# A gated recurrence that feeds a max-out feed-forward layer: the opening rearranged, the last rows stored by two queues

## The chip, the cores and the metric

The kernel runs on one core of a Trainium2 chip. The metric is device time in microseconds of one execution. Five executions of the kernel before took 400.87 to 401.7 us, median 401.0. The core's engines are TensorE (PE in the profile; PEld is its weight load), VectorE (DVE), ScalarE (ACT), GpSimd (POOL) and SyncE (SP). Each engine runs its own instructions in order. 16 DMA engines move data; transfers are issued by SP, ACT or POOL.

## The reference, cut to what matters

```python
# x, f_logit: (4, 6144, 256); lower_bound: (256)
f = lower_bound + (1 - lower_bound) * sigmoid(f_logit)
i = 1 - f
for t in range(6144):                      # for each of 4 batches
    h = f[:, t] * h + i[:, t] * x[:, t]
    y[:, t] = h
X = y.reshape(24576, 256)
out = np.maximum(X @ w1, X @ w2) @ w_out   # w1, w2: (256, 1024), w_out: (1024, 256)
```

All inputs and the output are float32.

## The kernel before

**Algebra.** With om = 1 - lower_bound and u = sigmoid(-f_logit), the forget factor is 1 - om·u and the input is om·u·x. The kernel scans with u·x as the drive, so the scan gives h/om, and folds om into the weights. The maximum is written as h1 + relu(h2 - h1): `wd` is om·(w2 - w1) in bf16, `rt` is relu(y·wd), and the output is rt·w_out + y·w13, where w13 = om·(w1·w_out) is a 256x256 matrix that the kernel computes in its opening. For that it needs w1 turned (`w1T`): `turn_w1` turns a quarter (256 of 1024 columns) by four TensorE transposes into PSUM, and `keep_w1` copies the quarter to SBUF as bf16.

**Tiling.** The 24576 tokens are 48 blocks of 512. For a block, 8 `hidden` steps (fc = 0 to 7) make one 128-column slice of y·wd each (two matmuls 128x512 into a PSUM tile `dT`) and evacuate it by a relu on ScalarE or VectorE. `project` then adds, for four groups of 128 tokens, 8 matmuls with `rt` and 2 with `y` into a PSUM tile `psO`; `store` copies two groups to SBUF (`osb`) and issues the output transfer on SP. In the main loop block j's hidden steps alternate with block j-1's project steps.

**Getting u, x and y turned.** The recurrence runs along the free dimension, so inputs must lie with channels on partitions. Blocks 0 to 2 are loaded as they are (`load`, tiles `fn`, `xn`), gated by ScalarE (`gate_nat`, `un`), multiplied by VectorE (`drive_nat`, `vn`) and turned by TensorE (`turn_pe`, PSUM tiles that come from the same pool of five as the hidden tiles). From block 3 on, chunks (block 3 alone, then pairs) are cast to bf16 into DRAM by DMAs issued on POOL (`cast`: `fs`, `xs`), turned by transposing DMAs issued on SP (`turn_dma`: `fT`, `xT`), gated by ScalarE (`gate`) and driven by VectorE (`drive`). `forget` makes the factors `ff` (ScalarE or VectorE), `scan` makes y (VectorE). Order between chunks: POOL copies one element of the last thing it must wait for into `held` and then issues the next cast. So the first cast waits for block 2's `fn` load (L520), and each later cast for the `fT` transpose of the chunk before (L389).

**The order around the change.** The order is written out by hand (`manual_schedule`), one list that gives each engine's order. The opening, L397 to L523, runs: loads on SP (weights by quarters, `w_out` by halves, blocks 0 to 2) and one load on ACT; a few filler matmuls (`keep_warm`); block 0 in two halves of 256 tokens, with the weight preparation quarter by quarter between (`diff` = w2 - w1 on POOL or VectorE, `scale` by om on ScalarE, `turn_w1`, `keep_w1`); block 1 in two halves; `linear_weights` and `keep_linear` for w13. The main loop from L525 starts with j = 1; within it block 2 is still gated, turned and scanned, between block 1's hidden steps (L537 to L551), block 0 is stored, and `gate_of` and `turn_of` say at which (block, step) a later block is gated and a chunk's transposes are issued.

**The end.** The last two groups of 128 tokens have a PSUM tile of their own; `store_row` copies half of the columns by VectorE and half by ScalarE into one tile and issues one transfer on SP.

Of the kernel before, what the change touches and what calls it, by code (L numbers as in the profile page):

```python
# [8 lines left out]
FP32 = mybir.dt.float32  # L9
# [7 lines left out]
def kernel(  # L17
# [42 lines left out]
    ypool = ctx.enter_context(tc.tile_pool(name="ypool", bufs=4))  # L60
    rpool = ctx.enter_context(tc.tile_pool(name="rpool", bufs=2 * FC + 4))
    opool = ctx.enter_context(tc.tile_pool(name="opool", bufs=4))
    PS = bass.MemoryType.PSUM
    ps_d = ctx.enter_context(tc.tile_pool(name="ps_d", bufs=5, space=PS))
    ps_o = ctx.enter_context(tc.tile_pool(name="ps_o", bufs=3, space=PS))
# [6 lines left out]
    nom = const.tile([P, KC], FP32)  # L72
    lbr = const.tile([KC, P], FP32)
    w1n = wpool.tile([P, KC, DFF], FP32)
    w2n = wpool.tile([P, KC, DFF], FP32)
    wdf = wpool.tile([P, KC, DFF], FP32)
    won = wpool.tile([P, FC, D], FP32)
# [13 lines left out]
    def load(j, s, q0, q1, eng=nc.sync):  # L91
        src = (f_logit, x)[s]
        eng.dma_start(
            out=ins[j][s][:, q0:q1, :],
            in_=src[0, j * TB + q0 * P : j * TB + q1 * P, :].rearrange(
                "(q p) d -> p q d", p=P
            ),
        )
# [18 lines left out]
    def turn_pe(j, s, q):  # L117
        if q == 0:
            (uT, vT)[s][j] = ps_d.tile([P, KC, TB], BF16, name="dT")
        dst, src = (uT, vT)[s][j], (us, vs)[s][j]  # L120
        for h in range(KC):
            nc.tensor.transpose(
                dst[:, h, q * P : (q + 1) * P], src[:, q, h * P : (h + 1) * P], ident_b[:]
            )
# [85 lines left out]
    def unit(fc):  # L210
        return slice(fc * P, (fc + 1) * P)
# [58 lines left out]
        n = FC + KC  # L270
        project_steps(j, i, half_ * n // 2, (half_ + 1) * n // 2)

    def store(j, g):
        osb = opool.tile([P, 2, D], FP32, name="osb")
        nc.vector.tensor_copy(out=osb[:], in_=pos[j, g, 0][:])  # L275
        r0 = j * TB + 2 * g * P
        nc.sync.dma_start(
            out=out[r0 : r0 + 2 * P, :].rearrange("(p r) d -> p r d", r=2), in_=osb[:]
        )

    def store_row(j, g, r):
        osb = opool.tile([P, 2, D], FP32, name="osb")
        ps = pos[j, g, r]
        nc.vector.tensor_copy(out=osb[:, 0, 0:P], in_=ps[:, 0, 0:P])
        nc.scalar.copy(out=osb[:, 0, P:D], in_=ps[:, 0, P:D])
        r0 = j * TB + 2 * g * P
        nc.sync.dma_start(
            out=out[r0 : r0 + 2 * P, :].rearrange("(p r) d -> p r d", r=2)[:, r, :],
            in_=osb[:, 0, :],
        )  # L290


    QF = DFF // 4

    def weight_load(k, w, src):
        cols = slice(k * QF, (k + 1) * QF)
        nc.sync.dma_start(  # L297
            out=w[:, :, cols], in_=src[:, cols].rearrange("(h p) f -> p h f", p=P)
        )
# [7 lines left out]
    def keeps():  # L307

        pt = ps_d.tile([P, TB], FP32, name="dT")
        nc.tensor.transpose(pt[:, 0:KC], lbr[:], ident[0:KC, 0:KC])  # L310
        nc.vector.tensor_scalar(
            out=om[:], in0=pt[:, 0:KC], scalar1=-1.0, scalar2=1.0, op0=ALU.mult, op1=ALU.add
        )
        nc.vector.tensor_scalar_add(out=nom[:], in0=pt[:, 0:KC], scalar1=-1.0)

    def diff(k, h0, h1, eng):
        cols = slice(k * QF, (k + 1) * QF)
        eng.tensor_tensor(  # L318
            out=wdf[:, h0:h1, cols],
            in0=w2n[:, h0:h1, cols],  # L320
            in1=w1n[:, h0:h1, cols],
            op=ALU.subtract,
        )
# [6 lines left out]

    pts = {}

    def turn_w1(k):
        pts[k] = ps_d.tile([P, 2, D], FP32, name="dT")
        for q in range(2):
            for h in range(KC):
                nc.tensor.transpose(
                    pts[k][:, q, h * P : (h + 1) * P],
                    w1n[:, h, unit(2 * k + q)],
                    ident[:],  # L340
                )

    def keep_w1(k):
# [24 lines left out]
    def keep_warm(n):  # L368
        for _ in range(n):
            nc.tensor.matmul(  # L370
                idle[:].rearrange("p r d -> p (r d)"),
                lhsT=warm[:, 0:P],
                rhs=warm[:],
                start=True,
                stop=True,
            )
# [3 lines left out]
    gate_of = {}  # L380
    for b, at in gate_at.items():
        gate_of.setdefault(at, []).append(b)
    turn_of = {(1, 3): 1}
    turn_of |= {(chunks[c][0] - 3, 5): c for c in range(2, NCH)}

    def cast_after_turn(c):
# [5 lines left out]
    with tc.manual_schedule():  # L392
# [1 line left out]
            alloc_in(j)  # L394


        nc.scalar.dma_start(out=lbr[:], in_=lower_bound.rearrange("(h p) -> h p", p=P))  # L397
        load(0, 0, 0, 2)
        load(0, 1, 0, 2, nc.scalar)
        for k in range(2):  # L400
            weight_load(k, w1n, moe_w1)
            weight_load(k, w2n, moe_w2)
            if k == 0:
                load(0, 0, 2, 4)
                load(0, 1, 2, 4)
        wout_load(0)
        for k in range(2, 4):
            weight_load(k, w1n, moe_w1)
            weight_load(k, w2n, moe_w2)
        for s in range(2):  # L410
            load(1, s, 0, 2)
        wout_load(1)
# [5 lines left out]
        nc.vector.memset(warm[:], 0.0)  # L418
        make_identity(nc, ident[:])
        nc.vector.tensor_copy(out=ident_b[:], in_=ident[:])  # L420
        keep_warm(6)
        keeps()
        keep_warm(2)


        gate_nat(0, 0, 2)
        drive_nat(0, 0, 2)
        for s in range(2):
            for q in range(2):
                turn_pe(0, s, q)  # L430
        forget(0, 0, 0, HB, on_act=True)
        forget(0, 1, 0, HB)
        for h in range(KC):
            scan(0, h, 0, HB)
        diff(0, 0, KC, nc.gpsimd)
        turn_w1(0)
        keep_warm(3)
        gate_nat(0, 2, 4)
        drive_nat(0, 2, 4)
        for s in range(2):  # L440
            for q in range(2, 4):
                turn_pe(0, s, q)
        scale(0, 0)
        forget(0, 0, HB, TB, on_act=True)
        forget(0, 1, HB, TB)
# [1 line left out]
        keep_w1(0)  # L447
        for fc in range(2):
            hidden_cols(0, fc, 0, HB)
        for h in range(KC):  # L450
            diff(1, h, h + 1, nc.gpsimd)
        for h in range(KC):
# [8 lines left out]
        for fc in range(2, 4):  # L461
            hidden(0, fc, on_dve=(fc == 3))
        keep_w1(1)
        for h in range(KC):
            diff(2, h, h + 1, nc.gpsimd)
        for h in range(KC):
            scale(2, h)
        for s in range(2):
            for i in range(4):
                project_steps(0, i, s, s + 1)  # L470
        turn_w1(2)
        for s in range(2, 4):
            for i in range(4):
                project_steps(0, i, s, s + 1)
        keep_w1(2)
        diff(3, 0, KC, nc.vector)
        for h in range(KC):
            scale(3, h)
        for fc in range(4, 6):
            hidden(0, fc, on_dve=(fc == 5))  # L480
        linear_weights(0, 4)
        turn_w1(3)
        gate_nat(1, 0, 2)
        drive_nat(1, 0, 2)
        keep_w1(3)


        for q in range(2):
# [26 lines left out]
            scan(1, h, HB, TB)  # L515
        for i in range(4):
            project_steps(0, i, 8, 10)


        nc.gpsimd.tensor_copy(out=held[:], in_=ins[2][0][:, NQ - 1, D - 1 : D])  # L520
# [4 lines left out]
        for j in range(1, NBLK + 1):  # L525
            if j == 2:
                for slot in range(4):
                    project(1, slot)
            for fc in range(FC):
                if j < NBLK:  # L530
                    hidden(j, fc, on_dve=(j == 1 and fc % 2 == 1))
                if j == 2:
                    if fc % 2:
                        project(1, 4 + fc // 2)
                elif j > 2:
                    project(j - 1, fc)
                if j == 1:  # L537
                    if fc == 0:
                        gate_nat(2, 0, NQ)
                        drive_nat(2, 0, NQ)  # L540
                        store(0, 0)
                    if fc == 3:
                        store(0, 1)
                    if fc in (5, 6):
                        for q in range(NQ):
                            turn_pe(2, fc - 5, q)
                    if fc == 7:
                        for h in range(KC):
                            forget(2, h, on_act=True)
                        for h in range(KC):  # L550
                            scan(2, h)  # L551
                if fc == 0 and j > 2:
                    store(j - 2, 1)
                if fc == 4 and 1 < j < NBLK:
                    store(j - 1, 0)
                if j == NBLK and fc in (3, 5, 7):
                    if fc == 3:
                        store(j - 1, 0)
                    else:
                        store_row(j - 1, 1, (fc - 5) // 2)  # L560
                for b in gate_of.get((j, fc), []):
                    gate(b)
                    drive(b)
                    for h in range(KC):
                        forget(b, h)
                        scan(b, h)
                c = turn_of.get((j, fc))
                if c is not None:
                    turn_dma(c)
                    if c + 1 < NCH:  # L570
                        cast_after_turn(c + 1)
# [30 lines left out]
```

## Time and profile before

| | |
|---|---|
| median of 5 executions | 401.0 us (400.87 to 401.7) |
| profiled execution | 400.91 us, span 399.1 us |
| PE busy | 388.8 us (97%) |
| PEld busy | 270.5 us (68%) |
| DVE busy | 249.1 us (62%) |
| ACT busy | 271.6 us (68%) |
| POOL busy | 45.3 us (11%) |
| DMA | 79.13 MB, mean 198 GB/s |
| granted TensorE clock | 0.999 |

The span is what the profiler recorded; 1.8 us of the execution lie around it. In lines of stages the columns are: the window, its length, then busy time and instructions of PE, PEld, DVE, ACT and POOL, the granted TensorE clock, the DMA engines' mean busy share (it can exceed 1, as packets of several queues overlap) and GB/s. In lines of waits: engine, line, what was waited for: total us, times, longest. In lines of the chain: start, length, what. In lines of the timeline: start, length, engine, line, operation, tiles, and in brackets the idle time before and what ended it. L259 is line 259 of the kernel.

### The profile page before, as it was taken

How to read it: one execution, taken by the hardware profiler on the slowest of the kernel's cores; microseconds unless marked ns; L12 is line 12 of the kernel's file. 1: busy time of each engine (PE TensorE's matmuls, PEld its weight loads, DVE VectorE, ACT ScalarE, POOL GpSimd, SP SyncE). 2: the span in 40 equal slices, each digit the busy share in tenths (PEclk: the TensorE clock that was granted, in tenths of full speed). 3: DMA queues.
4: the chain of work that ended last, by engine and by line, in shares of the span. 5: the costliest groups of instructions: out<-in, count | busy, mean ns of one | idle time of the engine just before them, and what ended most of it. 6: DMA issues, size and time to landing. Idle time of an engine off the chain costs nothing.

```text
span 399.1 us, 7240 instructions
## 1 busy us (share of the span) xinstructions
PE 388.8 (97%) x2784; PEld 270.5 (68%) x2784; DVE 249.1 (62%) x353; ACT 271.6 (68%) x450; POOL 45.3 (11%) x82
## 2 busy tenths in 40 slices
PE   7989999999999999999999999999999999999996
PEld 3656667766777667776677766777667766777664
DVE  4577656765676577557656765775676567657621
ACT  4846767666766776676677667666766776676661
POOL 2520111011012011020110110110201101100000
PEclk9999999999999999999999999999999999999999
DMA  8989999999999999899999999999999999995122
GB/s 258 348 161 186 221 225 248 218 200 212 192 208 208 210 192 225 188 180 233 194 183 218 204 189 216 196 221 198 178 226 191 190 214 206 191 217 145 54 103 83
DMA packets 126360, 79.13 MB, mean 198 GB/s; under 512 B 96243, under 2 KB 102645, under 8 KB 126325
## 3 DMA queue, kind: packets, MB, share of 16 engines
q1 hardware_dynamic: 113792, 54.80, 55.3%
q0 software_dynamic: 12256, 23.60, 36.6%
q8 instruction: 22, 0.36, 0.4%
q10 hardware_dynamic: 276, 0.26, 0.2%
q14 instruction: 14, 0.11, 0.1%
HBM read 53.48 MB, written 48.76 MB: 256 GB/s over the span
## 4 chain that ended last, share of the span: by engine, by line
PE 87%; DMA 10%; DVE 1%; POOL 0%; issue 0%; ACTq 0%; SPq 0%; ACT 0%; DVEq 0%; POOLq 0%
PE psO L259 49%; PE dT L221 38%; DMA xs<-in_x_dram 2%; DMA fn<-in_f_logit_dram 2%; DMA w2n<-in_moe_w_dram 2%; DMA xT<-xs 1%; DMA xn<-in_x_dram 1%; DMA fs<-in_f_logit_dram 1%; DMA fT<-fs 1%; DVE y L148 1%; DVE v L200 0%; POOL fs L172 0%; ACTq L397 0%; DVE ff L135 0%; SPq L297 0%
## 5 line engine op out<-in xcount | busy, mean ns | idle before, releaser
L236 ACT ACTIVATE rt<-dT 128x512 bf16<-128x512 f32 x376 | 219.0, 596 | 112.4 <-PE dT L221 111.9
L221 PE MATMUL dT<-y,wd 128*128 128x512 bf16 (+1 forms) x772 | 227.3, 378 | 3.2 <-DVE y L148 1.6
L259 PE MATMUL psO<-wob,rt 128*128 128x256 bf16 x1536 | 229.0, 273 | 0.2 <-DVE rt L234 0.2
L259 PEld LDWEIGHTS <-rt 128*128 128x128 bf16 x1536 | 150.2, 98 | 96.5 <-issue 0.8
L148 DVE TENSOR_TENSOR_SCAN y<-ff,y,v 128x512 bf16<-128x512 bf16 x84 | 107.8, 1284 | 3.0
L200 DVE TENSOR_TENSOR v<-u,xT 128x1024 bf16<-128x1024 bf16 x45 | 31.1, 691 | 100.1 <-ACT u L189 91.7
L221 PEld LDWEIGHTS <-wd 128*128 128x128 bf16 x772 | 75.2, 98 | 15.3 <-issue 3.6
L275 DVE COPY osb<-psO 128x512 f32<-128x512 f32 x95 | 64.4, 679 | 29.5 <-PE psO L259 29.4
L259 PE MATMUL psO<-w,y 128*128 128x256 bf16 x384 | 72.8, 273 | 0.0
L189 ACT ACTIVATE u<-fT 128x1024 bf16<-128x1024 bf16 x45 | 47.1, 1047 | 0.0
L389 POOL CAST held<-fT 128x1 f32<-128x1 bf16 x22 | 13.4, 608 | 287.4 <-DMA fT<-fs 287.4
L259 PEld LDWEIGHTS <-y 128*128 128x128 bf16 x384 | 37.5, 98 | 4.4
L135 DVE TENSOR_SCALAR ff<-u,nom 128x512 bf16<-128x512 bf16 x90 | 30.4, 338 | 0.0
L172 POOL DMA_DIRECT2D fs<-in_f_logit_dram x23 | 12.8, 558 | 2.3 <-issue 2.3
L172 POOL DMA_DIRECT2D xs<-in_x_dram x23 | 12.6, 550 | 0.0
L148 DVE TENSOR_TENSOR_SCAN y<-ff,v 128x512 bf16<-128x512 bf16 x6 | 7.3, 1225 | 0.2
L234 DVE TENSOR_SCALAR rt<-dT 128x512 bf16<-128x512 f32 x8 | 5.3, 688 | 2.5 <-PE dT L221 2.5
L110 DVE TENSOR_TENSOR vn<-un,xn 128x512 bf16<-128x512 bf16 (+1 forms) x5 | 4.0, 796 | 4.2 <-ACT un L103 2.7
L148 DVE TENSOR_TENSOR_SCAN y<-ff,y,dT 128x256 bf16<-128x256 bf16 (+1 forms) x8 | 6.6, 863 | 0.0
L370 PE MATMUL psO<-warm 128*128 128x512 bf16 x11 | 4.6, 558 | 1.2 <-DVE warm L418 1.2
L318 POOL TENSOR_TENSOR wdf<-w2n,w1n 128x256 f32<-128x256 f32 (+1 forms) x5 | 4.1, 837 | 7.7 <-DMA w2n<-in_moe_w_dram 7.7
L103 ACT ACTIVATE un<-fn 128x512 bf16<-128x512 f32 (+1 forms) x5 | 3.6, 714 | 2.0 <-DMA fn<-in_f_logit_dram 2.0
(34 smaller groups left out, 37.8 us busy)
## 6 DMA issues: line engine op xcount, KB each, us to landing
out_dram<-osb SPq DMA_DIRECT2D x95, 256.0 KB, 3.0
fs<-in_f_logit_dram POOLq DMA_DIRECT2D x22, 512.0 KB, 5.9
xs<-in_x_dram POOLq DMA_DIRECT2D x22, 512.0 KB, 9.2
fn<-in_f_logit_dram SPq DMA_DIRECT2D x4, 256.0 KB, 5.9
w1n<-in_moe_w_dram SPq DMA_DIRECT2D x4, 256.0 KB, 5.9
w2n<-in_moe_w_dram SPq DMA_DIRECT2D x4, 256.0 KB, 6.5
won<-in_moe_w_out_dram SPq DMA_DIRECT2D x2, 512.0 KB, 6.8
xn<-in_x_dram SPq DMA_DIRECT2D x3, 256.0 KB, 6.8
```

The costliest lines, as they stand in the source:

```text
L135: nc.vector.tensor_scalar(out=o, in0=i, scalar1=nom[:, h : h + 1], scalar2=1.0, op0=ALU.mult, op1=ALU.add)
L148: nc.vector.tensor_tensor_scan(out=ys[j][:, h, t0:t1], data0=ffs[j][:, h, t0:t1], data1=vT[j][:, h, t0:t1], initial=initial, op0=ALU.mult, ...
L172: nc.gpsimd.dma_start(out=t[0 : n * TB, :], in_=src[b, k * TB : (k + n) * TB, :], max_dma_last_dim=4096,)
L189: nc.scalar.activation(out=us[j][:], in_=chunk[c, 0][:, :, o * TB : (o + 1) * TB], func=AF.Sigmoid, scale=-1.0,)
L200: nc.vector.tensor_tensor(out=vT[j][:], in0=us[j][:], in1=chunk[c, 1][:, :, o * TB : (o + 1) * TB], op=ALU.mult,)
L221: nc.tensor.matmul(dts[j, fc][:, t0:t1], lhsT=wd[:, kc, unit(fc)], rhs=ys[j][:, kc, t0:t1], start=(t0 == 0 and kc == 0), stop=(t1 == TB an ...
L234: nc.vector.tensor_relu(out=rt[:], in_=dts[j, fc][:])
L236: nc.scalar.activation(out=rt[:], in_=dts[j, fc][:], func=AF.Relu)
L259: nc.tensor.matmul(ps, lhsT=lhsT, rhs=rhs, start=(s == 0 and (r == 0 or alone)), stop=(s == FC + KC - 1 and (r == 1 or alone)), skip_group ...
L275: nc.vector.tensor_copy(out=osb[:], in_=pos[j, g, 0][:])
L370: nc.tensor.matmul(idle[:].rearrange("p r d -> p (r d)"), lhsT=warm[:, 0:P], rhs=warm[:], start=True, stop=True,)
L389: nc.gpsimd.tensor_copy(out=held[:], in_=chunk[c - 1, 0][:, KC - 1, last : last + 1])
```

## The change

- `w1` is cast to bf16 by POOL (`round_w1`), and turned from there, into a bf16 PSUM tile.
- The second halves of w1 and w2 are loaded as one transfer each (512 columns, rows of 2 KB) instead of two quarters each. Quarters 2 and 3 are then prepared together: casts, turns and keeps in pairs; `diff(2)` goes from POOL to VectorE, `diff(3)` from VectorE to POOL; `linear_weights(0, 4)` goes ahead of hidden 4 and 5.
- `lower_bound` is loaded behind x's first half on the ACT queue, and `keeps` and the fillers stand at other places in PE's order.
- Block 2 is gated, driven, half turned and its forget factors made before block 1's main loop; its drive is turned behind hidden 1, its scans stand behind hidden 1 and 4. Block 1's relus on VectorE are 1, 4 and 6 instead of 1, 3, 5 and 7.
- Block 0's two stores are copied by ScalarE, behind hidden 5 and 7, instead of by VectorE behind hidden 0 and 3. The transposes of chunk 1 are issued behind hidden 7 instead of 3.
- `store_row` uses a tile for each half of the columns, and stores one by SP and one by the ACT queue.

```diff
+    lastpool = ctx.enter_context(tc.tile_pool(name="last", bufs=2))
...
+    w1b = wpool.tile([P, KC, DFF], BF16)
...
-    def store(j, g):
+    def store(j, g, on_act=False):
         osb = opool.tile([P, 2, D], FP32, name="osb")
-        nc.vector.tensor_copy(out=osb[:], in_=pos[j, g, 0][:])
+        if on_act:
+            nc.scalar.copy(out=osb[:], in_=pos[j, g, 0][:])
+        else:
+            nc.vector.tensor_copy(out=osb[:], in_=pos[j, g, 0][:])
...
     def store_row(j, g, r):
-        osb = opool.tile([P, 2, D], FP32, name="osb")
         ps = pos[j, g, r]
-        nc.vector.tensor_copy(out=osb[:, 0, 0:P], in_=ps[:, 0, 0:P])
-        nc.scalar.copy(out=osb[:, 0, P:D], in_=ps[:, 0, P:D])
         r0 = j * TB + 2 * g * P
-        nc.sync.dma_start(
-            out=out[r0 : r0 + 2 * P, :].rearrange("(p r) d -> p r d", r=2)[:, r, :],
-            in_=osb[:, 0, :],
-        )
+        dst = out[r0 : r0 + 2 * P, :].rearrange("(p r) d -> p r d", r=2)
+        low = lastpool.tile([P, P], FP32, name="low")
+        high = lastpool.tile([P, P], FP32, name="high")
+        nc.vector.tensor_copy(out=low[:], in_=ps[:, 0, 0:P])
+        nc.scalar.copy(out=high[:], in_=ps[:, 0, P:D])
+        nc.sync.dma_start(out=dst[:, r, 0:P], in_=low[:])
+        nc.scalar.dma_start(out=dst[:, r, P:D], in_=high[:])
...
-    def weight_load(k, w, src):
-        cols = slice(k * QF, (k + 1) * QF)
+    def weight_load(k, w, src, n=1):
+        cols = slice(k * QF, (k + n) * QF)
...
+    def round_w1(k):
+        cols = slice(k * QF, (k + 1) * QF)
+        nc.gpsimd.tensor_copy(out=w1b[:, :, cols], in_=w1n[:, :, cols])
+
     def turn_w1(k):
-        pts[k] = ps_d.tile([P, 2, D], FP32, name="dT")
+        pts[k] = ps_d.tile([P, 2, D], BF16, name="dT")
...
-                    w1n[:, h, unit(2 * k + q)],
-                    ident[:],
+                    w1b[:, h, unit(2 * k + q)],
+                    ident_b[:],
...
-    turn_of = {(1, 3): 1}
+    turn_of = {(1, 7): 1}
...
-        nc.scalar.dma_start(out=lbr[:], in_=lower_bound.rearrange("(h p) -> h p", p=P))
         load(0, 0, 0, 2)
         load(0, 1, 0, 2, nc.scalar)
+        nc.scalar.dma_start(out=lbr[:], in_=lower_bound.rearrange("(h p) -> h p", p=P))
...
-        for k in range(2, 4):
-            weight_load(k, w1n, moe_w1)
-            weight_load(k, w2n, moe_w2)
+        weight_load(2, w1n, moe_w1, 2)
+        weight_load(2, w2n, moe_w2, 2)
...
-        keep_warm(6)
-        keeps()
-        keep_warm(2)
+        keep_warm(7)
         gate_nat(0, 0, 2)
         drive_nat(0, 0, 2)
-        for s in range(2):
-            for q in range(2):
-                turn_pe(0, s, q)
+        for q in range(2):
+            turn_pe(0, 0, q)
+        keeps()
+        keep_warm(1)
+        for q in range(2):
+            turn_pe(0, 1, q)
         forget(0, 0, 0, HB, on_act=True)
         forget(0, 1, 0, HB)
         for h in range(KC):
             scan(0, h, 0, HB)
+        round_w1(0)
         diff(0, 0, KC, nc.gpsimd)
         turn_w1(0)
         keep_warm(3)
         gate_nat(0, 2, 4)
         drive_nat(0, 2, 4)
-        for s in range(2):
-            for q in range(2, 4):
-                turn_pe(0, s, q)
+        for q in range(2, 4):
+            turn_pe(0, 0, q)
+        keep_warm(1)
+        for q in range(2, 4):
+            turn_pe(0, 1, q)
...
+        round_w1(1)
         for h in range(KC):
             diff(1, h, h + 1, nc.gpsimd)
...
         keep_w1(1)
-        for h in range(KC):
-            diff(2, h, h + 1, nc.gpsimd)
-        for h in range(KC):
-            scale(2, h)
+        for k in (2, 3):
+            round_w1(k)
         for s in range(2):
             for i in range(4):
                 project_steps(0, i, s, s + 1)
-        turn_w1(2)
+        for k in (2, 3):
+            turn_w1(k)
         for s in range(2, 4):
             for i in range(4):
                 project_steps(0, i, s, s + 1)
-        keep_w1(2)
-        diff(3, 0, KC, nc.vector)
-        for h in range(KC):
-            scale(3, h)
+        for k in (2, 3):
+            keep_w1(k)
+        linear_weights(0, 4)
+        diff(2, 0, KC, nc.vector)
+        for h in range(KC):
+            diff(3, h, h + 1, nc.gpsimd)
+        for k in (2, 3):
+            for h in range(KC):
+                scale(k, h)
         for fc in range(4, 6):
             hidden(0, fc, on_dve=(fc == 5))
-        linear_weights(0, 4)
-        turn_w1(3)
         gate_nat(1, 0, 2)
         drive_nat(1, 0, 2)
-        keep_w1(3)
...
         for i in range(4):
             project_steps(0, i, 8, 10)
+        gate_nat(2, 0, NQ)
+        drive_nat(2, 0, NQ)
+        for q in range(NQ):
+            turn_pe(2, 0, q)
+        for h in range(KC):
+            forget(2, h, on_act=True)
...
-                    hidden(j, fc, on_dve=(j == 1 and fc % 2 == 1))
+                    hidden(j, fc, on_dve=(j == 1 and fc in (1, 4, 6)))
...
                 if j == 1:
-                    if fc == 0:
-                        gate_nat(2, 0, NQ)
-                        drive_nat(2, 0, NQ)
-                        store(0, 0)
-                    if fc == 3:
-                        store(0, 1)
-                    if fc in (5, 6):
+                    if fc == 1:
                         for q in range(NQ):
-                            turn_pe(2, fc - 5, q)
+                            turn_pe(2, 1, q)
+                        scan(2, 0)
+                    if fc == 4:
+                        scan(2, 1)
+                    if fc == 5:
+                        store(0, 0, on_act=True)
                     if fc == 7:
-                        for h in range(KC):
-                            forget(2, h, on_act=True)
-                        for h in range(KC):
-                            scan(2, h)
+                        store(0, 1, on_act=True)
```

## The prediction

> **What bounds the kernel now.** I first read the engines' shares (PE, the TensorE, is busy 97% of the span), then the stages, to see where the missing 3% lies.
>
> ```profile
> 5.00:10.00 5.00, 3.42 (x30) 2.16 (x29) 3.78 (x7) 2.90 (x6) 1.55 (x2) 1.00 1.09 358
> ...
> 50.00:100.00 50.00, 50.00 (x360) 35.06 (x359) 32.45 (x45) 35.15 (x58) 5.12 (x12) 1.00 1.08 220
> ...
> 390.00:399.20 9.20, 5.21 (x47) 4.32 (x45) 1.97 (x4) 1.15 (x4) 0.00 (x0) 0.94 0.25 88
> ```
>
> The second number after each window is PE's busy time. From 50 to 390 us PE never rests; over all such windows it is idle 6.5 us before 50, and 4 us in the last. So the time is fixed by the moment from which PE never rests again, plus the tail. PE's waits:
>
> ```profile
> PE dT L221 <- DVE y L148: 1.6, 4, 0.5
> PE dT L122 <- DVE vn L110: 1.6, 2, 1.1
> PE dT L221 <- DVE rt L234: 1.4, 1, 1.4
> ```
>
> The 1.4 us falls at 27.98, in block 1. But the timeline shows a later wait, the last one: 0.47 us at 46.82, for y of block 4. What PE wins before that point is lost there unless block 4's y comes sooner too. So the third view is the chain that leads to it.
>
> ```profile
> 12.67 7.51 DMA fn<-in_f_logit_dram
> ...
> 20.36 3.85 DMA fs<-in_f_logit_dram
> ...
> 24.23 3.40 DMA fT<-fs
> ...
> 28.75 9.58 DMA xs<-in_x_dram
> ...
> 38.35 4.49 DMA xT<-xs
> ...
> 46.82 0.38 PE dT L221
> ```
>
> From 12.67 to 42.84 this is transfers alone: block 2's load, the cast of chunk 0, its transpose, the cast of chunk 1 (issued once that transpose has landed), its transpose; then VectorE's 3.9 us for y. PE is only 0.47 us behind needing it: PE and this chain are nearly level, and the later of the two decides.
>
> **The change on PE's side (hidden if it gains, paid beyond a slack).**
> *w1 in bf16.* Four f32 transposes run 13.26 to 13.69, 0.43 us; eight bf16 ones 28.41 to 28.86, so four take 0.22. Four groups save 0.8 us of PE. Each round_w1 is a 128x512 cast on POOL: the 128x1024 casts took 1.04 and 1.44, so 0.52 to 0.72, and at worst 1.44; I take 0.65, four times 2.6 us. POOL stood idle 5.5 us ahead of the first difference, 1.7 ahead of the second and 3.0 ahead of the second wob cast, so the casts lie in waits for w2, except that the turn of quarter 3 now waits for its cast, at about 13.7.
> *14 to 18 us.* Both last differences now wait for all of w2's second half, and ScalarE gets in a row: two keeps (0.58 each), four scales (0.505 each), a relu (0.6), and only then block 1's gate (0.62), for which PE's transposes queue. With w2 in at 13.7 to 14.2 (before: 12.65 and 14.2 by quarters) and VectorE's difference 0.69, the scales end at 16.6 to 16.9, the gate at 17.8 to 18.1. PE transposed at 17.09 before, so it is 0.8 to 1.1 late, in spite of the transposes saved.
> *18 to 24 us.* A wait of 0.3 for the second wob cast goes (wob is ready earlier than PE). VectorE's scans of block 1 end near 23.8 (23.46 before): 0.3 late.
> *Block 2 ahead.* Its gate (1.05) moves in front of block 1 on ScalarE, 8 transposes on PE and two forgets (0.69 each) too; block 1's relus queue behind the forgets until about 25.1, while PE needs the first buffers back only at 26. VectorE then has, without pause: drive 1.23, relu 0.69, scan 1.26, relu 0.69, scan 1.26, relu 0.69, together 5.8, ending at 29.6. It loses two store copies (1.37) and a relu; ScalarE gets them (0.60 each, by its relus of that size; its casts out of PSUM took 0.58) ahead of block 3's gate, which ends near 30.9 against 31.3, so nothing waits. The 1.37 us wait at 27.98 goes, for that relu now stands behind one drive and no copy; what is late next is PE's project of block 1 on the last VectorE relu, about 1 us. But block 2's scans are then long over, and its hidden starts near 31.1 instead of waiting until 32.73: PE is about 1.4 us ahead.
> So PE reaches block 4 near 45, with 1.9 us of slack on the old chain (1.4 and the 0.47). All these gains are worth nothing beyond the chain's own.
>
> **The change on the chain's side (what sets the time).**
> *Load order.* x's first half is issued 0.58 us sooner, as lbr no longer stands ahead of it on ScalarE's queue. The 16 DMA engines were at 0.83 and 1.00 in the windows 2 to 3 and 3 to 4, so there was little room: between 0 and -0.58, I take -0.15. lbr now lands behind x, but its first user waits for x anyway.
> *2 KB rows.* Four quarters (1.05 MB) of 1 KB rows become two transfers of 2 KB rows, all ahead of block 2's load in the same queue.
>
> ```profile
> 9.00:10.00 1.00, 1.00 (x10) 0.79 (x11) 0.94 (x2) 0.87 (x2) 0.28 (x1) 1.00 1.09 348
> ```
>
> The last number is GB/s: from 8 to 20 us 1 KB rows move at 346 to 350 with the engines full. The DMA rate from 380 us on, where only output stores run, whose rows are 2 KB:
>
> ```profile
> GB/s 277 192 354 0 0 0 0 0 0 145 375 26 0 0 0 0 0 90 388 68 0 0 0 0 0 30 388 162 0 0 209 337 152 122 51 222 0 0 0 17
> ```
>
> Its full slices show 375 and 388. At 348 the 1.05 MB take 3.01 us, at 388 2.70: -0.31, or 0 if rows don't matter to loads. I take -0.31, by the store rows.
> The Trainium skill's page "DMA: Bandwidth & Descriptors" (Specifications) speaks against it: about 358 GB/s is the limit of HBM for one core, and 348 is nearly there, so longer rows would bring some 0.08 us. Yet this trace moves 375 GB/s of 1 KB rows between 6 and 7 us, above that limit; by the rule the sum below would end 0.23 higher.
> *First stores.* store(0,0) was issued at 27.36 and its bytes moved before chunk 1's cast began to flow (25 GB/s at 29.0 to 29.5). Now it follows ScalarE's copy, at about 28.7, and store(0,1) at about 29.9 (29.15): both lie beside the cast, whose xs is on the chain and in whose time the engines are full. A store is 256 KB, at 388 GB/s 0.68 us: between 0 (it fits the gap of 0.39 and 0.73 share at 29.0 to 29.5 and 30.0 to 30.5) and +0.68. I take +0.2, since most of that gap is open to it.
> *Chunk 1's transposes* move from behind hidden 3 to behind hidden 7. On SyncE's queue they now follow store(0,1), gone at 30; they wait until 34.0 for fs in any case, and POOL's next cast waits for their landing as before: 0.
> *Tail.* The two copies of a row took turns:
>
> ```profile
> 395.25 0.29 DVE L284 COPY osb<-psO 128x128 f32<-128x128 f32 x1 [0.80 <-PE psO L259]
> 395.57 0.27 ACT L285 COPY osb<-psO 128x128 f32<-128x128 f32 x1 [0.82 <-DVE osb L284]
> ```
>
> Two tiles part them if the wait is over osb: -0.32. But they also read one PSUM tile, and disjoint parts of one SBUF tile are used together elsewhere (VectorE writes the second half of y from 9.41 while PE reads the first), so I take it to stay. Then the low half leaves 0.3 us sooner, the high half at the same moment, half the bytes (-0.17 at 388), but by ScalarE's queue, whose issues took 0.43 to 0.54 against 0.33: +0.1 to +0.2, and in 512 B rows. I take -0.1, ends -0.4 and +0.3.
> The skill's page "PSUM — Partial Sum Buffer" (PSUM bank collisions raise a hardware error) says that two engines must not be in one bank at once, reads included, so the turn would remain; no run here shows it broken up. By it the tail stays at -0.1.
>
> **Sum.** -0.15 - 0.31 + 0.2 - 0.1 = -0.36 us. The profiled execution took 400.91 (span 399.1 and 1.8 around it); the median is 401.0, so 400.6. The bounds add to -1.3 and +1.0.
>
> **Rivals.**
> *Faster by more.* The store fits the gap, the early load brings 0.3, and the copies part: -0.15 more, -0.2 and -0.3, about 399.9. For it: the gap in the DMA rows; against: the PSUM tile shared.
> *The change doesn't do what it says to the loads.* Rows don't matter, the store costs its 0.68, the tail is level: 401.0 + 0.68 - 0.15 = 401.5. For it: full DMA engines from 30.5 to 36; against: 388 GB/s.
> *Slower: ScalarE's line at 14 to 18 us takes the place of the waits removed.* If block 1's gate slips not by 0.9 but by 2.8 us or more (slower POOL casts beside VectorE, keeps behind a late quarter 3, scales behind these), everything through VectorE's 5.8 us moves with it; beyond the 1.9 us of slack each us is one of the total. A slip of 4 gives about 402.1. For it: eight ScalarE instructions in a row with nothing between; against: PE waits there and later that would take up part.
>
> **How the numbers follow.** A measurement of this kernel can tell about 0.2%, 0.8 us. Forecast: 0.42, between 400.2 and 401.1, so all within 0.2%. Faster rival: 0.32, of which 0.30 below 400.2. Loads rival: 0.13, 401.2 to 401.9, a third of it over 401.8. Slower rival: 0.13, over 401.8. So faster 0.30, same 0.53, slower 0.17. The range 399.7 to 401.9 holds the forecast, the loads rival and two thirds of the faster rival, and leaves out about 2 in 10; the forecast's own range is 400.2 to 401.1.
>
> **What would show it.** Right: PE's wait for block 4's y grows from 0.47 to more than 1 us and stays the last one; block 2's fn lands 0.4 earlier than 20.18; the 1.4 us wait for rt is gone; xs of chunk 1 takes 9.6 to 10 us; in the last row ScalarE's copy still follows VectorE's. Wrong: no wait at block 4 (PE is the later one, and the walk from 14 us is off), or fn2 at its old time. Also the fillers: six of them run at 0.43 us each, three at 7.28 within 0.81, so PE is slow at first; if the pause after the seventh filler keeps it slow past 9 us, PE's side is later than worked out.

## The result, and the profile after

The changed kernel took 403.3 us (median of 22 executions, 401.38 to 404.92) against 401.06 before (43 executions): a ratio of 1.0048, 95% interval 1.0037 to 1.0059. It is slower by half a percent; the forecast was 400.6, in a range of 399.7 to 401.9. The profiled execution took 401.88 us, span 400.0, so it is one of the quicker ones, 0.97 us above the profiled execution of before.

The waits of PE in the changed kernel (engine, line, cause: total us, times, longest):

```profile
PE dT L223 <- DVE y L150: 2.7, 3, 1.2
PE dT L124 <- ACT un L105: 1.5, 2, 1.0
...
PE psO L261 <- DVE rt L236: 0.6, 1, 0.6
```

The 1.4 us wait for a relu of VectorE is gone, and 0.6 us in the project of block 1 took its place. Block 1's gate now makes PE wait 1.0 us. But the longest waits are for y, and the timeline of PE has them where the old one of 0.47 us was, at block 4:

```profile
46.17 0.39 PE L223 MATMUL dT<-y,wd 128*128 128x512 bf16 x1 [1.11 <-DVE y L150]
47.74 0.38 PE L223 MATMUL dT<-y,wd 128*128 128x512 bf16 x1 [1.17 <-DVE y L150]
```

PE stopped at 45.06, did one matmul, and went on at 47.74, 0.92 us later than the 46.82 of before. From there to the end nothing differs, so these 0.92 us are the 0.9 of the span. The chain that leads there:

```profile
11.41 8.64 DMA fn<-in_f_logit_dram
...
20.22 3.72 DMA fs<-in_f_logit_dram
...
23.96 3.61 DMA fT<-fs
...
28.16 5.63 DMA fs<-in_f_logit_dram
...
33.81 4.76 SPq L186
...
38.66 5.08 DMA xT<-xs
...
47.74 0.38 PE dT L223
```

Up to the second cast (28.16, against 28.20 before) it is level. Then it loses: SyncE is 4.76 us with chunk 1's first transpose (3.93 before), the second is issued at 38.66 instead of 38.35, and it takes 5.08 (4.49). The later issue (0.3) and the longer transpose (0.6) are the 0.9 us. The median lies 1.4 us higher still, and the mean granted clock of the executions says where to look: the 8 with a clock of 0.998 or more took 401.38 to 402.8 us (median 401.9), the 14 with 0.993 to 0.996 took 403.12 to 404.92 (median 403.75). Below, "kept their clock" and "lost it" stand for these two groups.

### The profile page after: what moved, and what is told of

It is laid out like the page before. It is cut to its first block, busy times and chain, and to the rows that moved or that the text cites. A ratio compares the mean times of both kernels' runs of the same rounds, so it can differ in the third digit from the quotient of the medians.

```text
span 400.0 us, 7238 instructions
## 1 busy us (share of the span) xinstructions
PE 389.6 (97%) x2785; PEld 270.5 (68%) x2785; DVE 247.8 (62%) x350; ACT 273.0 (68%) x453; POOL 45.9 (11%) x86
## 4 chain that ended last, share of the span: by engine, by line
PE 87%; DMA 8%; SPq 2%; DVE 1%; issue 0%; POOL 0%; ACT 0%; DVEq 0%; POOLq 0%
PE psO L261 49%; PE dT L223 38%; DMA fs<-in_f_logit_dram 2%; DMA fn<-in_f_logit_dram 2%; DMA w1n<-in_moe_w_dram 1%; DMA xT<-xs 1%; SPq L186 1%; SPq L95 1%; DMA fT<-fs 1%; DVE y L150 1%; SPq L303 0%; DVE v L202 0%; DVE ff L137 0%; DVE low L293 0%; ACT high L294 0%
## 5 line engine op out<-in xcount | busy, mean ns | idle before, releaser
L202 DVE TENSOR_TENSOR v<-u,xT 128x1024 bf16<-128x1024 bf16 x45 | 31.1, 692 | 103.1 <-ACT u L191 94.5
L280 DVE COPY osb<-psO 128x512 f32<-128x512 f32 x93 | 63.0, 679 | 30.1 <-PE psO L261 30.1
L399 POOL CAST held<-fT 128x1 f32<-128x1 bf16 x22 | 11.5, 524 | 290.3 <-DMA fT<-fs 290.3
L380 PE MATMUL psO<-warm 128*128 128x512 bf16 x12 | 5.9, 630 | 1.2 <-DVE warm L427 1.2
L133 ACT ACTIVATE ff<-dT,nom 128x256 bf16<-128x256 bf16 (+1 forms) x7 | 3.5, 532 | 3.7 <-PE dT L124 2.5
```

The lines of the kernel that those rows point to most:

```text
L202: nc.vector.tensor_tensor(out=vT[j][:], in0=us[j][:], in1=chunk[c, 1][:, :, o * TB : (o + 1) * TB], op=ALU.mult,)
L380: nc.tensor.matmul(idle[:].rearrange("p r d -> p (r d)"), lhsT=warm[:, 0:P], rhs=warm[:], start=True, stop=True,)
L399: nc.gpsimd.tensor_copy(out=held[:], in_=chunk[c - 1, 0][:, KC - 1, last : last + 1])
```

## The experiments

All were run beside the kernel before, in three groups, in which its medians were 401.4 (the first four kernels), 401.12 (the next four) and 401.09 us (the last two). Theory A: PE is ahead of the chain of transfers; the chain is later by the moved stores; and while PE waits for it the clock is lowered. Theory B: the time is lost in PE's own opening.

### The changed kernel again

No edit.

> The changed kernel again, unchanged, to time it beside the others and to look at another of its executions. Theory A (chain and clock): the wait for block 4's y stays near 1.2 us at 47 to 48 in the trace, PE idles some 2.5 us around it, and executions at 403 us or more have a mean granted clock of 0.993 to 0.996, lost directly behind that wait. Theory B (opening): the lost clock lies elsewhere, before 30 us, where the fillers were moved. Both: about 403.3 us, ratio about 1.005.

Measured: 404.09 us (6 executions), ratio 1.0051 (1.0031 to 1.0071); five of the six had a clock of 0.994 to 0.996, and this time the profiled execution was one of them (404.25, span 402.3). Its stages around block 4 (window, length, busy time and instructions of PE, PEld, DVE, ACT, POOL, granted clock, DMA share, GB/s):

```profile
46.00:47.00 1.00, 0.11 (x1) 0.11 (x2) 1.00 (x2) 0.38 (x1) 0.00 (x0) 1.00 1.03 172
47.00:48.00 1.00, 0.28 (x1) 0.00 (x1) 0.96 (x2) 0.00 (x0) 0.00 (x0) 1.00 1.11 166
48.00:49.00 1.00, 0.55 (x2) 0.25 (x2) 1.00 (x3) 0.00 (x0) 0.00 (x0) 0.62 1.11 209
49.00:50.00 1.00, 1.00 (x7) 0.71 (x5) 0.96 (x3) 0.60 (x1) 0.00 (x0) 0.50 1.11 203
50.00:51.00 1.00, 1.00 (x5) 0.39 (x4) 1.00 (x1) 0.01 (x1) 0.00 (x0) 0.50 1.01 275
51.00:52.00 1.00, 1.00 (x7) 0.68 (x6) 0.96 (x3) 0.59 (x1) 0.00 (x0) 0.67 1.13 196
52.00:53.00 1.00, 1.00 (x9) 0.71 (x8) 1.00 (x2) 0.60 (x1) 0.00 (x0) 1.00 1.05 221
```

and PE's timeline there:

```profile
46.89 0.39 PE L223 MATMUL dT<-y,wd 128*128 128x512 bf16 x1 [1.12 <-DVE y L150]
48.45 0.59 PE L223 MATMUL dT<-y,wd 128*128 128x512 bf16 x1 [1.17 <-DVE y L150]
48.83 1.27 PE L261 MATMUL psO<-wob,rt 128*128 128x256 bf16 x5
...
52.18 0.71 PE L261 MATMUL psO<-wob,rt 128*128 128x256 bf16 x5
```

The clock column falls below 1 just before PE gets its y, and stays at half for 0.76 + 1 + 1 + 0.66 = 3.4 us: the same five matmuls take 1.27 us instead of 0.71. Half speed for 3.4 us costs up to 1.7 us; here it costs 1.6, as PE still waits for the first 0.2. The opening is no slower than in the other execution: a filler takes 0.38 us at 8.37 here, and 0.63 at 8.53 there. The waits themselves are those of the other execution (1.12 and 1.17). But the lower clock isn't the whole difference of 2.3 us between the two spans: block 4 also starts 0.71 us later (48.45 against 47.74), because block 2's f landed 0.71 us later (the first copy to `held` starts at 20.81 instead of 20.10).

### Fillers while PE waits

```diff
+    def fill(n):
+        pt = ps_d.tile([P, TB], FP32, name="dT")
+        for _ in range(n):
+            nc.tensor.matmul(pt[:], lhsT=warm[:, 0:P], rhs=warm[:], start=True, stop=True)
...
+            if j == NP + 1:
+                fill(10)
             for fc in range(FC):
```

> The changed kernel with 10 filler matmuls of 512 columns (2.1 us) on PE ahead of block 4's hidden steps, so that PE works while it waits for y. Nothing else moves, and the output stays as it is. Theory A: y of block 4 is no earlier (47.7), but the clock is no longer lowered behind the wait: all executions at about 401.8, clock 0.998 to 1.0, so 1.5 us faster than the changed kernel's median. Theory B: no effect, median about 403.3.

Measured: 402.25 us (12 executions, 401.09 to 403.09), ratio 1.0017 (1.0006 to 1.0027). All twelve had a clock of 0.998 or more. So 1.8 us of the 404.09 in the same group were the clock, and what lowers it is PE's rest at block 4 and nothing earlier: for this part theory B falls. The other 0.85 us over the kernel before stay. It is 0.4 above the expected 401.8, and why isn't settled: the traced execution, at 402.91, is itself 0.66 above the median. In it block 2's f landed 0.4 later than in the changed kernel's, and from the first copy to `held` to block 4's drive it took 24.3 us against 23.7.

### Block 0's stores behind chunk 1's transposes

```diff
-        nc.sync.dma_start(
-            out=out[r0 : r0 + 2 * P, :].rearrange("(p r) d -> p r d", r=2), in_=osb[:]
-        )
+        if on_act:
+            late.append((j, g, osb))
+        else:
+            send(j, g, osb)
...
                     turn_dma(c)
+                    while late:
+                        send(*late.pop(0))
```

> The changed kernel with block 0's two stores issued on SyncE behind chunk 1's two transposes instead of ahead of them, so no store moves beside chunk 1's cast; the copies stay where they are. Theory A with the stores as cause of the later chain: chunk 1's xs lands 0.7 us sooner, y of block 4 is ready near 47.0 instead of 47.7, the span is 0.4 to 0.7 shorter, and the shorter idle time lowers the clock less often. Rival: the chain is later for another reason (the engines' order, the load), and y of block 4 stays at 47.5 or later.

Measured: 400.95 us (12 executions), ratio 0.9988 (0.9974 to 1.0002), clock 0.998 or more in all. Block 2's f lands at different times in different executions (the first copy to `held` starts at 20.06 to 20.82 us in the traces of kernels that load it as the changed one does and wait for it), so I read the chain from the second copy to `held`, which releases chunk 1's cast, to block 4's drive. Before:

```profile
27.75 0.19 POOL L389 CAST held<-fT 128x1 f32<-128x1 bf16 x1 [6.18 <-DMA fT<-fs]
42.93 0.69 DVE L200 TENSOR_TENSOR v<-u,xT 128x1024 bf16<-128x1024 bf16 x1 [3.89 <-DMA xT<-xs]
```

In the changed kernel:

```profile
27.70 0.19 POOL L399 CAST held<-fT 128x1 f32<-128x1 bf16 x1 [6.26 <-DMA fT<-fs]
43.84 0.69 DVE L202 TENSOR_TENSOR v<-u,xT 128x1024 bf16<-128x1024 bf16 x1 [5.86 <-DMA xT<-xs]
```

With the stores late:

```profile
28.14 0.19 POOL L407 CAST held<-fT 128x1 f32<-128x1 bf16 x1 [5.98 <-DMA fT<-fs]
42.41 0.69 DVE L202 TENSOR_TENSOR v<-u,xT 128x1024 bf16<-128x1024 bf16 x1 [3.72 <-DMA xT<-xs]
```

That is 15.18, 16.14 and 14.27 us: without stores beside the cast it takes 1.9 us less than with two. Other traces repeat the first two figures: 15.32 with the stores where they were (the tail alone, below), and 16.15, 15.98 and 16.05 where the change puts them (the changed kernel again, rows of 1 KB, the first cast earlier). In the kernel before, the first store was issued at 27.36, 0.4 us ahead of that copy, and each landed in 2.1 us; in the changed one it was issued at 28.92, 1.2 us behind the copy, and the two took 7.2 and 8.9 us to land. So the stores beside the cast cost the chain, and the 0.96 us fit their new place. The gain is larger than expected (0.7).

### Block 2 back at its old place

```diff
-        gate_nat(2, 0, NQ)
-        drive_nat(2, 0, NQ)
-        for q in range(NQ):
-            turn_pe(2, 0, q)
-        for h in range(KC):
-            forget(2, h, on_act=True)
...
+                    if fc == 0:
+                        gate_nat(2, 0, NQ)
+                        drive_nat(2, 0, NQ)
+                        store(0, 0)
+                    if fc == 3:
+                        store(0, 1)
+                    if fc in (5, 6):
+                        for q in range(NQ):
+                            turn_pe(2, fc - 5, q)
```

with `turn_of`, the relus and the scans as before.

> The changed kernel with one part undone: block 2's gate, turns, forgets and scans, block 0's stores and chunk 1's transposes stand where they stood before (copies by VectorE behind hidden 0 and 3). Theory A: PE comes later to block 4, so its wait there is under 0.7 us, the stores run ahead of the cast and y of block 4 is ready near 46.7; about 401.0, clock 0.998 or more. If the time lost lay in the first 20 us (theory B, or ScalarE's line at 14 to 18 us), it stays: about 402.5 to 403.5.

Measured: 401.38 us (12 executions), ratio 1.0005 (0.9993 to 1.0016), no clock under 0.998. The time is as expected, but one reason was not: the trace has y of block 4 not at 46.7 but at 48.16, the drive 16.6 us after the copy to `held`. The rest of the opening is later than before, so the first store was issued at 28.10, 0.45 us behind the copy at 27.65, and it too lay beside the cast. But 16.6 us are more than the 16.14 of the changed kernel, whose stores are later still, so the stores' place alone doesn't explain this chain; and the traced execution took 402.24, 0.86 above the median, so the usual chain of this kernel is probably shorter, which no trace shows. PE waited 1.1 us there, less than in the changed kernel since it came later, and kept its clock. By the times, this part of the change (block 2 early, the stores later, and what goes with them) accounts for all that the change loses, 404.09 against 401.38; which of the two loses what, this run doesn't part.

### The first cast released earlier

```diff
-        nc.gpsimd.tensor_copy(out=held[:], in_=ins[2][0][:, NQ - 1, D - 1 : D])
+        nc.gpsimd.tensor_copy(out=held[:], in_=ins[1][0][:, NQ - 1, D - 1 : D])
```

> The changed kernel with the first cast released by block 1's second f load instead of block 2's f load (one index in the copy to held), about 2 us sooner; nothing else. Theory A (the chain of transfers sets the time and PE is ahead of it): the whole chain moves 1 to 2 us forward, the wait for block 4's y falls below 0.5 us or goes, the clock stays at 0.998 or more, and the time falls to 400.0 to 401.0. Rival (PE's own opening, ScalarE's line at 14 to 18 us, sets the time): y of block 4 comes sooner but the time stays at 401.8 or more.

Measured: 401.68 us (12 executions), ratio 1.0019 (1.0005 to 1.0034). The first cast was issued at 17.73 instead of 20.22, but its transpose at 23.24 instead of 23.96: beside the loads the cast takes longer (5.49 us against 3.72), and the chain gained 0.7 us, not 1 to 2. PE rested 2.1 us between 40 and 50 instead of 2.3, and now 9 of 12 executions kept their clock (400.79 to 401.95) while 3 lost it (0.993 and 0.994: 403.27 to 403.54). One program, two groups 2.0 us apart by their medians, and the clock tells which. The expectation of 400.0 to 401.0 was missed: from the second copy to `held` (27.10) to block 4's drive (43.15) it still takes 16.05 us, with the stores beside the cast.

### Both edits

> Both edits to the changed kernel: block 0's stores issued behind chunk 1's transposes, and the first cast released by block 1's load. Theory A: y of block 4 is ready 3 to 4 us sooner than in the changed kernel, so PE doesn't wait for it at all and the opening is bounded by PE itself: about 399.6 to 400.4, faster than before. If the chain of transfers weren't what binds, no faster than 401.

Measured: 399.67 us (5 executions, 399.05 to 400.07), ratio 0.9961 (0.9949 to 0.9973): faster than both kernels. PE in the windows from 40 to 50, of the changed kernel:

```profile
40.00:45.00 5.00, 5.00 (x37) 3.34 (x35) 1.13 (x3) 4.16 (x7) 1.27 (x3) 1.00 1.10 244
45.00:50.00 5.00, 2.72 (x18) 1.67 (x18) 4.93 (x7) 1.86 (x4) 0.00 (x0) 1.00 1.07 176
```

and with both edits:

```profile
40.00:45.00 5.00, 5.00 (x37) 3.45 (x36) 4.09 (x6) 4.24 (x7) 0.00 (x0) 1.00 1.06 215
45.00:50.00 5.00, 5.00 (x38) 3.52 (x37) 4.93 (x8) 3.13 (x6) 0.00 (x0) 1.00 1.12 227
```

The wait at block 4 is gone, and PE's own opening is the bound. Block 4's drive starts at 40.84, 3.0 us sooner than in the changed kernel, and waits for ScalarE's gate, no longer for the transpose.

### Rows of 1 KB again

```diff
-        weight_load(2, w1n, moe_w1, 2)
-        weight_load(2, w2n, moe_w2, 2)
+        for k in range(2, 4):
+            weight_load(k, w1n, moe_w1)
+            weight_load(k, w2n, moe_w2)
```

> The changed kernel with one part undone: the second halves of w1 and w2 loaded as four quarters of 1 KB rows. If rows of 2 KB are quicker (prediction: 0.31 us): block 2's f lands 0.1 to 0.4 later after the first issue than in the changed kernel, DMA moves 348 instead of 359 GB/s between 10 and 15 us, time within 0.4 us of the changed kernel's. If rows don't matter: no difference in either.

Measured: 403.47 us (5 executions), ratio 1.0059 (1.0047 to 1.0071), as the changed kernel's 403.3. The rows do move faster, 350 GB/s here between 10 and 15 us against 358 to 368 in the traces with rows of 2 KB. But a gain on the chain isn't shown. Block 2's f releases `held` at 20.25 here, and at 20.23 and 20.24 in the two traces of the old loads (before, the tail alone); with rows of 2 KB it is 20.10, 20.81, 20.52, 20.82 and 20.06 (changed kernel, again, fillers, late stores, block 2 back). Where this spread of 0.76 us comes from is open. PE rested 2.4 us at block 4, and all five executions lost their clock (0.994 to 0.996).

### The tail alone

The kernel before with the new `store_row` and nothing else.

> The kernel before with only the tail changed: two tiles for the halves of the last rows, one stored by SyncE and one by ScalarE's queue. Prediction: between -0.4 and +0.3 us, -0.1 taken, because ScalarE's copy still waits for VectorE's. So 401.0 within 0.3 of the kernel before. If the two queues' completion costs more at the end, up to +0.5.

Measured: 401.09 us (12 executions), ratio 1.0006 (0.9996 to 1.0016): no difference. In the last row of this kernel ScalarE's copy still follows VectorE's, and its store is issued last:

```profile
395.60 0.29 DVE L289 COPY low<-psO 128x128 f32<-128x128 f32 x1 [0.80 <-PE psO L260]
395.93 0.27 ACT L290 COPY high<-psO 128x128 f32<-128x128 f32 x1 [0.82 <-DVE low L289]
396.23 0.35 ACTq L292 DMA_DIRECT2D out_dram<-high  x1
```

The two copies write different tiles now, so the turn isn't over the SBUF tile; what they still share is the PSUM tile that both read. No run gives each a PSUM tile of its own.

### The two edits without the change, and with it again

The kernel before with the late stores and the early cast; and the kernel of "both edits" a second time.

> The kernel before with the two edits to the transfers alone (block 0's stores issued behind chunk 1's transposes, the first cast released by block 1's f load) and nothing of the change. Theory A: the wait for block 4's y (0.47 us) goes, and PE's own opening is then the bound, so the gain is about that 0.5 us: 400.4 to 400.8. If the gain of e6_late_early came from the transfers alone and PE's side of the change were worth nothing, it would be as fast as that kernel, 399.7.

> The kernel of e6_late_early again, beside the other on one chip: 399.7, ratio to before 0.996. Theory A: 0.8 to 1.4 us faster than e9_before_both, what PE's side of the change is worth once the transfers come in time.

Measured, on one chip: 400.53 us (12 executions), ratio 0.9983 (0.9972 to 0.9994), and 399.69 us (6 executions), ratio 0.9955 (0.9939 to 0.9971). The transfers alone bring 0.56 us, about the 0.47 that PE waited at block 4; with the change it is 1.4. So PE's side of the change is worth 0.84 us once the transfers come in time, and less than nothing while they don't.

## Why the prediction was wrong

**What bounds the kernel: right.** PE never rests after block 4's y, and the later of PE and the chain decides.

**PE's side: right, nearly step by step.** Block 1's gate ended at 18.13 (17.8 to 18.1 worked out), PE's transposes for it came at 18.18 (17.9 to 18.2), the wait for a relu of VectorE went and 0.6 us of the expected 1 came in its place, block 2's hidden began at 31.44 (31.1), and PE reached block 4 at 45.06 (45). Its slack on the old chain was 1.76 us (45.06 to 46.82; 1.9 worked out), and 1.4 us of gain on the kernel before showed when the chain was moved. The sign named for a late PE, fillers still slow near 9 us, came in the profiled execution (0.63 us at 8.53) and cost nothing at block 4.

**2 KB rows and load order: not shown to gain.** Worked out were -0.31 and -0.15 on the chain. In the pair of profiled executions block 2's f landed at 20.05 instead of 20.18, -0.13 for both, but over five traces with the new loads it landed between 0.17 sooner and 0.6 later than with the old ones. The rate rose to 359 GB/s in the stage from 10 to 15 us and not to the 388 of the stores, and the later loads went on at 348. The limit of about 358 in the Trainium skill's page "DMA: Bandwidth & Descriptors" (Specifications) was nearer than the row of stores, though 359 and, in another of these runs, 368 GB/s are over it.

**First stores: the first step that failed.** It was put at +0.2, at most +0.68, by one store's bytes at the full rate. Measured: +0.96 from before to after, and 1.9 for both stores beside the cast, whose bytes at that rate are 1.35. So the stores cost the chain more than their bytes. On the cast it is about what was put: xs landed 9.9 us after its issue, before 9.58. What the term left out are the transposes behind the cast: SyncE's issue of the first took 4.76 us (3.93 before, 3.89 with the stores late), the flight of the second 5.08 (4.49 and 4.3). Block 4's +0.92 us is this term.

**The clock: the step that is missing.** The prediction foresaw a wait of more than 1 us at block 4, even named it as the sign of being right, and counted it as free. The sum has no term for it. It isn't free: after PE's rest of 2.3 us the clock is at half for 3.4 us in most executions (19 of 28), and PE is the bound there, so it costs up to 1.7 us. With the chain's 0.9 that is 2.6 over the 401.06 of before, and the executions that lost their clock lie 2.7 over it (median 403.75); the others lie 0.8 over it (401.9). The median of all, 2.2 over it, is among the former. The trace of before had a hint, its fillers at 0.43 us against 0.21 later, and I used it only for the start.

**Tail: right.** -0.1 was taken; no difference was measured (401.09 against 401.12), and the copies take turns.

**The rivals.** The slower rival had the wrong place: ScalarE's line at 14 to 18 us did slip as worked out, and PE's slack took it. The loads rival came nearest in its mechanism (the rows bring nothing and the store costs all it can), at 401.5 against the 401.9 of executions that kept their clock. No rival had the clock. (The terms of the faster rival add up to 400.0, not 399.9.)

## What to carry to other kernels

When an engine is made to arrive earlier at a wait that something else ends, ask two things: whether the work moved to get there lands beside the transfers that end the wait, and what the longer rest does to the engine's clock. A TensorE that comes a little later and rests less (block 2 back, 401.38 us) can be faster than one that comes early and waits (404.09). And an edit that is worthless or worse alone (PE ahead by 1.3 us, at 45.06 instead of 46.35) can become the better part of a gain when the transfers are moved with it, as the 399.7 us show.

## What the runs showed of the hardware that was not expected

A short rest is enough to lower TensorE's clock. Between 40 and 50 us PE rested, in the trace of each kernel, for 0.3 us (late stores), 0.8 (fillers) and 1.1 (block 2 back): no execution of these, 36 in all, had a mean clock under 0.998. At 2.1 us (early cast) 3 of 12 did, at 2.3 (the changed kernel) 19 of 28, at 2.4 (1 KB rows) 5 of 5. In the traced case the rest was two waits of 1.1 and 1.2 us with a matmul between.

Why the same rest loses the clock in one execution and not in another comes out of the traces' records of the clock. Apart from the last, which the end cuts off, the stretches of one clock last whole multiples of 3.413 us: in the changed kernel again, full from 3.88, half from 48.25 (44.37 us, 13 times 3.413), full again from 51.66; in the changed kernel, full from 9.33 to 398.44 (389.12 us, 114 times). Cut into such pieces, PE's rest lies over two of them in the profiled execution of the changed kernel, and both pieces and what follows are at full clock:

```profile
43.46:46.87 3.41, 1.99 (x14) 1.11 (x13) 2.96 (x5) 2.21 (x4) 0.00 (x0) 1.00 1.09 179
46.87:50.29 3.42, 2.55 (x19) 1.82 (x19) 3.38 (x5) 1.38 (x3) 0.00 (x0) 1.00 1.06 190
```

In the changed kernel again most of it lies in one, and the next is at half:

```profile
44.84:48.25 3.41, 1.32 (x8) 0.60 (x7) 3.34 (x5) 1.54 (x3) 0.00 (x0) 1.00 1.07 175
48.25:51.66 3.41, 3.21 (x13) 1.82 (x13) 3.34 (x7) 1.19 (x2) 0.00 (x0) 0.50 1.06 229
```

PE is idle (the piece's length less PE's busy time) for 1.42 and 0.86 us of the first two pieces, and for 2.09 of the third. The other traces agree: after 2.45 us idle in a piece (1 KB rows, 44.95 to 48.37) the clock is at half, after 1.71 (early cast, 44.94 to 48.35) it isn't; at the end of the kernels it falls after pieces with 2.07 us idle or more and not after 1.69. So in these traces the limit lies between 1.71 and 2.07 us of rest in one piece of 3.41, and where the pieces begin differs by execution.

The Trainium skill's page "TensorE: Matmul & The Clock Gate" (Part 1: The HAM clock gate) has the clock go to half after an idle window of about 3.4 us, and these windows run free of the kernel. The 3.41 us pieces, and that the same rest loses the clock in some executions only, agree with that. That 2.09 us of rest in a window suffice doesn't agree with its rule "no PE-idle gaps >~3.4µs" (the same part, HAM oscillation), if that is read as letting shorter gaps pass.

What stays open: executions of the kernel before had a mean clock of 0.994 to 0.996 too, 6 of 29 in the first group, 5 of 23 in the second and 2 of 16 in the third. Most cost nothing: the five of the second group took 400.78 to 401.48 us, beside a median of 401.12. No trace shows where those lost it, so a low mean clock alone doesn't show lost time.
